# Decayed attention and a small mixture of experts on one core: another split of keys and queries, other constants, another order of the work

## The chip, the cores and the metric

One core of one Trainium2 chip runs the whole program. The time is the device time of one launch in microseconds (us); a kernel's time is the median of its runs. TensorE is called PE here, its weight loads PEld, VectorE DVE, ScalarE ACT, GpSimd POOL, and the queue that issues every transfer of this kernel SP.

## The reference

There are 8 batches, 8 heads, 576 positions and a head size of 64. First comes causal attention with a decay per position, then a mixture of four small attention experts on its result, of which each position uses two:

```
scores = q @ k.T / 8                                    # per batch and head, 576 x 576
cum    = cumsum(log(clip(f, 1e-4, 1)))                  # decay of the head
scores = where(j > i, -1e9, scores + cum[i] - cum[j])
attn   = softmax(scores) @ v                            # x: 8 x 576 x 512, heads side by side

logits = x @ w_gate ; top-2 of 4 experts, softmax over the two -> w
for e in 0..3:
    qe, ke, ve = x @ wq[e], x @ wk[e], x @ wv[e]
    ye = softmax(causal(qe @ ke.T / 8)) @ ve @ wo[e]
    out += w[e] * ye          where e is one of the two
```

## The kernel before, in words

The unit of work is a pair: two heads of a batch (32 pairs, kind "a") or two experts of a batch (16 pairs, kind "m"). Products are made exact enough by splitting each operand into a rounded high part (type fp32r, made by an ACT copy) and a low part (the rest, made by a DVE subtraction); a product is high times high plus the two mixed ones.

A pair goes through these tasks. Each is a Python generator; each `next` on it emits the instructions up to its next `yield`, and that is called a step.

- `prep_attn` (L372): loads keys and queries of both heads from DRAM into `xin` (one transfer of 576 KB into 64 of the 128 partitions; the two halves of `xin` alternate from pair to pair), rounds the keys and the queries with two ACT copies into 64 partitions ("near") of the tile `kq` (L380), reads two or three rows of constants, decay and -1 into the other 64 partitions ("far") of `kq` (`extra_rows`, L358), makes the two low parts with DVE into the tile `ka` (L387), and copies the two high parts into `ka`, to the partitions where its second matmul operand needs them, with two transfers of 288 KB (`copy_bits`, L370). There are four `kq` buffers and three `ka` buffers.
- `max_pass` (L536): an approximate product (high parts and far rows of `kq` alone, contraction over 128 partitions) for the maximum of each row. PE writes blocks of scores to two PSUM buffers (L546), DVE reduces them (L552, L565), PE turns the ten columns of maxima into rows (`mp`, L609), ACT negates them (L612), and two small transfers write them into one far row of `kq` (`ms`, L370). Only then can the scores start.
- `scores` (L639): exact scores by two matmuls a block, `ka` (L643) and `kq` (L644), in two PSUM buffers; ACT takes the exponential (L660 to L698), POOL zeroes what lies above the diagonal (L630, L663, L700) and adds up the rows for the softmax sums (L706 to L712).
- `attend` (L721): 14 matmuls (28 in the trace, since plain fp32 is done in two passes; L731) of values and probabilities.
- per two pairs `row_sums` (L762) and `apply_rows` (L813) divide by the sums. For a batch's experts come besides `moe_front` (values and gate, L422), `prep_moe` (keys and queries of the experts, L518) and `project_out` (L864), whose result SP stores.

At the start there are `decay_rows` (the logarithms and their cumulative sum), `spread_rows` (writes the rows of decay and constants to a DRAM table `ex`, from which `extra_rows` reads all pairs but the first), `load_weights` (nine pieces of the experts' weights, three steps each: load, ACT copy, POOL subtraction, L346) and `constants` (POOL).

What sets the order is a string, `ORDER`. Two of its digits (base 64) name a task in a list of 292; the tasks are advanced by one step each time their number stands in the string, 5285 steps in all. At the end every instruction is bound to follow the one emitted before it on its engine (L925 to L930). So each engine, and SP's queue of transfers, does its work strictly in the string's order, and an instruction that waits holds up everything behind it on its own engine; engines run ahead of each other as far as data and buffers allow.

`warm` (L182) multiplies a tile of zeros, to no effect on the result. 35 such products stand at the very start (L271 to L274). More are bound to steps of the first three pairs (`WARM`, L380 and L387): those are emitted right behind the copy or subtraction of `prep_attn` and wait for it (`together`).

Of the kernel before, what the change touches and what calls it, by code (L numbers as in the profile page):

```python
# [11 lines left out]
F32 = mybir.dt.float32  # L12
F32R = mybir.dt.float32r
# [38 lines left out]
1b1f1f1d1p1p1f1f1f16161b1b1b1b1b1b1b1b1b1b1b161m1m1m1m1k1k1k1k1l1p1w1y1p1p1p0q1p1p1p1p1p1p1m1m1p1m1m1m1p0c1b1c1c
1g1g1g1g1g1g17171m17171g1g1m1k1k171l1c1m1m0i1m1g1g1g1g1g1g1g1p1p1p1k1k1m1m1717171w1g1g1g0Q1g1g1g1g1g1g1m1k1x171m
161m1p1p1m1m1m1p1p1p1p1w1p1p1p1p1p1g1g1g1p1p1g1g1g1g0u1m1m1m1p1m1m1w1p1h1h1q1q1q1q1p0X0X1q1w1q1w1w0X0X1n17171n1n
1n1n1p171h1q1q1q1i1i1q1i1q1B1q1i1i171i1n1n1n1q1n1n1i0b0b1q0X0X1n0X0X1n1q1i1n1n1n1i1q1q0X0W1n1n1n1n1q1q1q1I1q1q1n
1n1n1n1n1n1y1n1n1n1n1n1j1j0X0X1q1q1q1q1q1j1y1B1y1B1x1B1o1B1o1y1n1r1r1r1y1y1y1y1N1B1B1D1r1r1r0X0X1i1y1j1j1y1y1y1y
1r1r1r1r1y1r1r1o1y1y1r0V1y1y1y1r0X0X1y1y1y1j1j1r1r1r1r1r1r1r1r1r1r1r1r1r1D1D1C1y0W1y1r1y1D1I1j1r1r1j1j1j1y1D1D1I
1D1r1j1D1c1D1s1j1D1z1D1D1D1D1z1z1z1z1I1z1D1z1D1D1z1z1z1I1z151K1K1K1z1z1K1t1t1D1D1z1z1z1z1D1D1D1D101s1U1U1U1U1K1t
1t1t1s1K1N1t1t1U1U1z1z1z1z1z1z1t1z1z1z0U1D1D1J1t1U1U1U1U1U1U1U1U1V1D1I1D1D1U1U1U1m1t1U1K1U1U1U1U1U1K1K1U1z1u1u1E
1E1E1E1E1N1z1N1N1u1u1K1K1K1K1K1u1u1u1z1u1E1E1E1A1u1u1u1N1E1E1E1K1K1U1U1E1E1E1u1u1E1q1E1I1I1K1U1U1U1K1K1K1d1K1z1z  # L60
1i1U1V1V1K1K111U1V1V1E1U1U1U1U1U1U1U1U1u1u1u1u1N1V1E1E1V1E1E1E1E1E1K1K1K1E1E1E1E1E1A1A1W1V1V1E1K1E1V1P1P1N1U241V
1V0+1V1V1F1F1P1P1V1V1F1P1V1V1V1V1V1V1K1V1P1P1P1P1V1w1V1V1V1L1L1L1L0X1o1L1P1P1L1P1P1U1G1G1V1L1V1O1P1P1G1G1P1P1P1L
1L1L1L1L1G1L1L1L291G1P1P1P1V1P1V1P1V1L1V1V1V1V1L1L1L0L1P1P1P1Z1P1P1G1G241L1L1L1L1L1L1L0n1Z1Z0A1Z1W1G1V1Z1W1W1U1U
# [64 lines left out]
def tile_decay_attention_moe(ctx: ExitStack, tc, qk, v, f, w_gate, wq, wk, wv, wo, out):  # L128
    nc = tc.nc
# [52 lines left out]
    def warm(at, cols, after=None, n=None):  # L182

        for i, r in enumerate(at):
            k = slice(r, r + (n or 128 // len(at)))
            mm = nc.tensor.matmul(wps[i][:, :cols], wz[k, 0:128], wz[k, :cols], start=True, stop=True)  # L186
            if after is not None:
                together(mm, after)
# [25 lines left out]
    for _ in constant_rows(0, nc.vector):  # L214
        pass
# [756 lines left out]
```

## Time and profile before

| | |
|---|---|
| median of 3 runs | 722.81 us (721.54 to 724.28) |
| the profiled execution | 721.82 us, its span 719.9 us |
| PE busy | 687.3 us, 95% of the span, 5373 instructions |
| DVE busy | 575.9 us, 80% |
| POOL busy | 469.3 us, 65% |
| ACT busy | 445.2 us, 62% |
| transfers | 72.81 MB, mean 101 GB/s |
| mean granted PE clock | 0.981 |

The span runs from the first to the last instruction. Matmuls are pipelined, so a stretch in which PE is busy throughout need not be a stretch at its full rate; the time in which PE stands idle, and what ended the idle time, is read from the stretches and from the timeline. The granted clock of a stretch is given as a share of 2.4 GHz.

### The profile page before, as it was taken

The page shows a single profiled execution, that of the slowest core. Times are in us where ns is not written, and L with a number is a line of the kernel's source. Part 1 is how long each engine was busy: PE and PEld are TensorE (multiplying, and loading weights), DVE is VectorE, ACT ScalarE, POOL GpSimd, SP SyncE. Part 2 cuts the span into 40 slices and gives each one's busy share as a digit, 9 for nine tenths or more (in the row PEclk, how much of TensorE's full clock was granted, in tenths as well). Part 3 has the DMA queues.
Part 4 walks back from the last instruction along what each step waited for, and adds up shares of the span by engine and source line. Part 5 has one row for each costly group of instructions (what it writes and reads, how often), then busy time and mean ns, then how long its engine had stood idle before and what let it go on. Part 6 is the DMA issues. An engine that isn't in the chain of part 4 may idle for free.

```text
span 719.9 us, 15408 instructions
## 1 busy us (share of the span) xinstructions
PE 687.3 (95%) x5373; PEld 559.8 (78%) x5373; DVE 575.9 (80%) x1666; ACT 445.2 (62%) x959; POOL 469.3 (65%) x767
## 2 busy tenths in 40 slices
PE   8788899999999999999999999999999999999997
PEld 4466688768787798788878788877988788979864
DVE  6678976897888888897988888788987987866662
ACT  4465756666576665676576765766666675556443
POOL 8799864687556865766655946667657776465270
PEclk9588999999999999999999999999999999999999
DMA  7756343362254425263262643353444324112103
GB/s 166 204 117 177 78 112 94 73 157 54 57 135 113 122 54 135 55 166 96 56 159 74 155 88 103 69 146 99 106 118 102 101 73 100 39 48 64 34 30 117
DMA packets 29469, 72.81 MB, mean 101 GB/s; under 512 B 4169, under 2 KB 4649, under 8 KB 27345
## 3 DMA queue, kind: packets, MB, share of 16 engines
q1 hardware_dynamic: 29393, 71.84, 40.3%
q8 instruction: 42, 0.69, 0.4%
q14 instruction: 34, 0.28, 0.1%
HBM read 32.91 MB, written 10.35 MB: 60 GB/s over the span
## 4 chain that ended last, share of the span: by engine, by line
PE 68%; POOL 10%; DVE 9%; ACT 5%; DMA 4%; issue 3%; SPq 0%; POOLq 0%; DVEq 0%; ACTq 0%
PE pp_m L518 10%; PE pv L422 7%; PE ob_a L731 6%; PE s_a L643 6%; PE m_a L546 5%; PE po L864 5%; PE s_a L644 5%; PE s_m L643 4%; PE m_m L546 3%; PE s_m L644 3%; PE oa_a L731 3%; POOL R_m L706 3%; PE sm_a L771 2%; PE warm L186 2%; POOL R_m L708 2%
## 5 line engine op out<-in xcount | busy, mean ns | idle before, releaser
L630 POOL TENSOR_SCALAR_AFFINE_SELECT P_a<-P_a 128x128 f32<-128x128 f32 x128 | 45.9, 361 | 107.0 <-ACT P_a L693 59.6
L552 DVE CUSTOM_DVE_ANT_0 junk_a<-m_a,mask 128x320 bf16<-128x320 f32 (+2 forms) x192 | 93.2, 485 | 26.6 <-PE m_a L546 18.2
L643 PE MATMUL s_a<-ka_a 128*128 128x320 f32 (+4 forms) x384 | 111.1, 313 | 1.5 <-ACT P_a L660 0.9
L644 PE MATMUL s_a<-kq 128*128 128x320 f32 (+4 forms) x384 | 104.6, 299 | 0.7 <-DMA kq<-ms_a 0.7
L546 PE MATMUL m_a<-kq 128*128 128x320 f32 (+4 forms) x384 | 93.4, 316 | 7.2 <-DVE mxs_a L552 4.0
L387 DVE TENSOR_TENSOR ka_a<-xin,kq 64x1152 fp32r<-64x1152 f32 x64 | 96.2, 1503 | 2.5 <-ACT kq L380 1.0
L526 ACT ACTIVATE kq<-pp_m 64x288 fp32r<-64x288 f32 x128 | 51.8, 405 | 62.6 <-DVE ka_m L528 43.4
L528 DVE TENSOR_TENSOR ka_m<-pp_m,kq 64x288 fp32r<-64x288 f32 x128 | 58.3, 455 | 34.5 <-ACT kq L526 32.4
L643 PEld LDWEIGHTS s_a<-ka_a 128*128 128x128 f32 (+1 forms) x384 | 70.9, 185 | 14.6 <-ACT P_a L660 4.6
L380 ACT ACTIVATE kq<-xin 64x1152 fp32r<-64x1152 f32 x64 | 73.0, 1157 | 11.1 <-DMA xin<-in_qk_dram 10.4
L706 POOL TENSOR_TENSOR R_a<-P_a 128x448 f32<-128x448 f32 x64 | 78.7, 1230 | 0.0
L546 PEld LDWEIGHTS m_a<-kq 128*128 128x128 f32 (+1 forms) x384 | 63.9, 186 | 18.1 <-DVE mxs_a L552 8.0
L644 PEld LDWEIGHTS s_a<-kq 128*128 128x128 f32 (+1 forms) x384 | 70.5, 185 | 1.8 <-DMA kq<-ms_a 0.9
L731 PE MATMUL ob_a<-P_a,va 128*64 128x320 f32 (+1 forms) x512 | 68.8, 411 | 0.0
L708 POOL TENSOR_TENSOR R_a<-R_a,P_a 128x320 f32<-128x320 f32 x64 | 65.2, 1019 | 4.9
L660 ACT ACTIVATE P_a<-s_a 128x512 f32<-128x512 f32 x64 | 36.6, 597 | 34.7 <-PE s_a L644 33.8
L643 PE MATMUL s_m<-ka_m 128*128 128x192 f32 (+2 forms) x192 | 54.7, 309 | 1.1 <-ACT P_m L660 0.9
L731 PEld LDWEIGHTS ob_a<-P_a,va 128*64 128x64 f32 x512 | 36.4, 140 | 24.9 <-issue 1.4
L552 DVE CUSTOM_DVE_ANT_0 junk_m<-m_m,mask 128x192 bf16<-128x192 f32 (+2 forms) x96 | 46.5, 485 | 9.3 <-PE m_m L546 6.3
L644 PE MATMUL s_m<-kq 128*128 128x192 f32 (+2 forms) x192 | 51.3, 294 | 1.5 <-DMA kq<-ms_m 1.5
L663 POOL TENSOR_SCALAR_AFFINE_SELECT P_a<-P_a 128x256 f32<-128x256 f32 x64 | 32.5, 519 | 30.9 <-ACT P_a L660 30.2
L630 POOL TENSOR_SCALAR_AFFINE_SELECT P_m<-P_m 128x128 f32<-128x128 f32 x64 | 19.7, 310 | 44.4 <-ACT P_m L678 29.8
(189 smaller groups left out, 2069.8 us busy)
## 6 DMA issues: line engine op xcount, KB each, us to landing
xin<-in_qk_dram SPq DMA_DIRECT2D x32, 576.0 KB
ka_a<-kq SPq DMA_DIRECT2D x64, 288.0 KB
va<-in_v_dram SPq DMA_DIRECT2D x32, 320.0 KB
ka_m<-kq SPq DMA_DIRECT2D x32, 288.0 KB
out_dram<-outb SPq DMA_DIRECT2D x32, 256.0 KB
kq<-ex SPq DMA_DIRECT2D x47, 27.0 KB
kq<-ms_a SPq DMA_DIRECT2D x64, 2.5 KB
out_dram<-outb SPq DMA_DIRECT2D x8, 128.0 KB
```

The costliest lines, as they stand in the source:

```text
L380: made = nc.scalar.activation(hi[near], x[:, 2 * c : 2 * c + 2], AF.Copy)
L387: made = nc.vector.tensor_tensor(lo, x[:, 2 * c : 2 * c + 2], hi[near].bitcast(F32), ALU.subtract)
L518: nc.tensor.matmul(pp[:, :HS], w[:, c, es], x[c][:, gs], start=(n == 0), stop=(n == 3 * KC - 1))
L528: nc.vector.tensor_tensor(lo[:, h, gs], src, hv.bitcast(F32), ALU.subtract)
L546: nc.tensor.matmul(dst, qB[0:K, h, i0 : i0 + dst.shape[0]], kB[0:K, h, j0:j1], start=True, stop=True)
L552: nc.vector.tensor_tensor_reduce(jk[:, :n], src, mask[:, MW - n :], 1.0, init, ALU.add, ALU.max, acc)
L630: return nc.gpsimd.affine_select(pv, pv, [[1, 128]], ALU.is_ge, 0.0, base=0, channel_multiplier=-1)
L643: nc.tensor.matmul(dst, kaf[:, c : c + m], qA[:, h, i0:i1], start=True, stop=False)
L644: nc.tensor.matmul(dst, kqf[0:K, c + h * S : c + h * S + m], qB[0:K, h, i0:i1], start=False, stop=True)
L706: g.tensor_tensor(r[:, h, 128:S], q[:, 320:768], q[:, 768:1216], ALU.add)
L708: g.tensor_tensor(r[:, h, 256:S], r[:, h, 256:S], q[:, 1216:1536], ALU.add)
L731: mm = nc.tensor.matmul(dst[64 * h : 64 * h + 64, c0 : c0 + rhs.shape[-1]], vs[h][0:kp, blk], rhs, start=first, stop=last,)
```

## The change

- Layout. The host lays out keys and queries of a pair as 128 rows of two heads: for one pair the keys in rows 0 to 63 and the queries in rows 64 to 127, for the next the other way round, so that keys land in the pair's near rows and queries in its far rows. `xin` becomes a tile of the pool `work` with two buffers.
- High parts. ACT rounds the keys into `kq` (near) as before, and the queries now into `ka` (far). The queries' place in `kq` (near) is filled from `ka` by ACT for the first two pairs (`NACT`), and by a transfer of 288 KB for all others. This transfer stands ahead of `extra_rows`; the second one, keys from `kq` to `ka`, stays at the end.
- Constants. The rows of -1 are set for the first pair's `kq` alone. The selectors `sel` are written directly by memsets; eight `affine_select`s, the buffer they used (shared with `max_pass`) and two DVE copies go.
- Zero products. `warm` and `WARM` go. A task `keep_warm` with 50 products of zeros (bf16, 128 x 128 by 128 x 512) takes their place, one a step, which the order can put anywhere; they wait for nothing but the memset of their operand.
- `junk`, which DVE's reductions write and nobody reads, gets a second buffer.
- `ORDER` is another string: 293 tasks, 5328 steps.

```
-ORDER (5285 steps)   4w4w4w4z004z02054x4w4w4w4y00004x4x0000...
+ORDER (5328 steps)   004x4x4x4x004w4x00004y4y4y4y4y4A4A4y4x...
-WARM = (1, 1, 1)
+NWARM = 50
+NACT = 2
...
-    xin = const.tile([128, 4, S], F32, name="xin")
...
+    wz = const.tile([128, 512], BF16, name="wz")
+    nc.vector.memset(wz, 0.0)
+
+    def keep_warm():
+        wps = ptile(ps_o, "o", "warm")
+        for _ in range(NWARM):
+            nc.tensor.matmul(wps, wz[:, 0:128], wz, start=True, stop=True)
+            yield
...
-        nc.gpsimd.memset(kq[far.start : far.start + 2, :, 1].bitcast(F32), -1.0)
-
+        if i < DIRECT:
+            nc.gpsimd.memset(kq[far.start : far.start + 2, :, 1].bitcast(F32), -1.0)
...
-            sf = work.tile([128, 128], F32, tag="mx0", name=f"self{p}")
-            nc.gpsimd.memset(sf, 0.0)
+            nc.gpsimd.memset(sel[p].bitcast(F32), 0.0)
             for h in range(2):
-                blk = sf[:, 64 * h : 64 * h + 64]
                 base = 32 * (2 * p + h)
-                for r in range(2):
-                    nc.gpsimd.affine_select(
-                        blk, blk, [[0, 64]], ALU.not_equal, 1.0, base=-(base + r), channel_multiplier=1
-                    )
-                    yield
-            yield
-            nc.vector.tensor_copy(sel[p], sf)
-            yield
+                nc.gpsimd.memset(sel[p][base : base + 2, 64 * h : 64 * h + 64].bitcast(F32), 1.0)
+                yield
...
-        x = xin[near]
+        x = work.tile([128, 2, S], F32, tag="xin", name="xin" + nm, bufs=2)
         nc.sync.dma_start(x, qk[b, hp])
         yield
-        for c, hi in ((1, kB), (0, qB)):
-            made = nc.scalar.activation(hi[near], x[:, 2 * c : 2 * c + 2], AF.Copy)
-            if u["first"] is not None:
-                for _ in range(WARM[u["first"]]):
-                    warm((0, 64), 512, made)
+
+        for hi, at in ((kB[near], near), (qA[far], far)):
+            nc.scalar.activation(hi, x[at], AF.Copy)
             yield
+        if u["i"] < NACT:
+            nc.scalar.activation(qB[near], x[far], AF.Copy)
+        else:
+            copy_bits(qB[near], qA[far])
+        yield
         yield from extra_rows(u, b * NPH + hp)
-        for c, hi, lo in ((1, kB, kA[far]), (0, qB, qA[near])):
-            made = nc.vector.tensor_tensor(lo, x[:, 2 * c : 2 * c + 2], hi[near].bitcast(F32), ALU.subtract)
-            if u["first"] is not None:
-                for _ in range(WARM[u["first"]]):
-                    warm((0,), 512, made)
+        for lo, hi, at in ((kA[far], kB[near], near), (qA[near], qA[far], far)):
+            nc.vector.tensor_tensor(lo, x[at], hi.bitcast(F32), ALU.subtract)
             yield
         copy_bits(kA[near], kB[near])
         yield
-        copy_bits(qA[far], qB[near])
-        yield
...
-            jk = work.tile([128, MW], BF16, tag="junk", name="junk" + nm)
+            jk = work.tile([128, MW], BF16, tag="junk", name="junk" + nm, bufs=2)
```

Read by tasks, the two orders begin like this (steps of a task in brackets; "a0_0" is batch 0, pair 0):

- before, on PE: 35 zero products, then `max_pass` a0_0 with the zero products of pairs 0, 1 and 2 in between, the first block of a0_1's `max_pass`, `mp` of a0_0, more of a0_1, `scores` a0_0. On DVE the subtractions of pair 1 stand behind the first of the two 448-column reductions of a0_0, those of pair 2 behind the second one of a0_1. On SP: `f`, a weight, pair 0, pair 1, then the table `ex`, the decay rows of pair 0, and the rest.
- after, on PE: 36 zero products, all blocks of `max_pass` a0_0, 12 zero products, the first block of a0_1, `mp` of a0_0, more of a0_1 with one zero product, `scores` a0_0. On DVE the subtractions of pair 1 stand behind the 320-column reduction of a0_0, those of pair 2 behind the one of a0_1. On SP: `f`, pair 0, two weights, pair 1, two weights, the decay rows of pair 0, then the table `ex`. On POOL the subtractions of all weights and the last constants stand ahead of the third mask of a0_0's `scores`; before, three weight subtractions and the last constants stood behind the scores of a0_0.
- from batch 1 on, the same tasks follow each other in nearly the same sequence; the steps within them are placed differently.

## Rows read from the trace of the kernel before

**Rows 1.** Busy time by stretch: PE, PEld, DVE, ACT, POOL, clock, DMA share, GB/s

```profile
13.90:26.10 12.20, 7.54 (x25) 4.26 (x24) 8.15 (x24) 2.22 (x2) 8.45 (x11) 0.65 0.99 238
...
40.80:88.40 47.60, 42.27 (x297) 29.57 (x296) 41.38 (x107) 30.40 (x62) 42.90 (x67) 0.93 0.56 135
90.00:684.00 594.00, 581.97 (x4750) 488.70 (x4748) 491.00 (x1461) 379.68 (x834) 378.26 (x629) 1.00 0.39 96
```

**Rows 2.** Timeline of PE: start, length, engine, line, tiles, count, idle before

```profile
13.77 0.87 PE L546 MATMUL m_a<-kq 128*128 128x192 f32 x4
...
19.71 0.80 PE L186 MATMUL warm<-wz 128*128 128x512 f32 x1 [2.69 <-DVE ka_a L387]
...
29.77 0.36 PE L643 MATMUL s_a<-ka_a 128*128 128x192 f32 x1
...
40.81 0.87 PE L731 MATMUL oa_a<-P_a,va 128*64 128x256 f32 x8
...
88.40 0.87 PE L731 MATMUL oa_a<-P_a,va 128*64 128x256 f32 x8
```

**Rows 3.** The chain of work in order of time, from its start to 27 us

```profile
1.53 12.45 PE warm L186 x36
...
15.17 7.29 DMA xin<-in_qk_dram
22.49 2.22 ACT kq L380 x2
24.76 0.79 PE warm L186 x2
...
26.33 0.23 PE mp_a L609
```

**Rows 4.** The same chain at its end

```profile
709.37 6.83 PE po L864 x27
```

**Rows 5.** Zero products by their shapes, 1.5 to 13.9 us

```profile
L186 PE MATMUL warm<-wz 128*128 128x512 f32 x8 | 5.2, 731 | 1.5 <-DVE wz L179 1.5
```

**Rows 6.** Timeline of DVE

```profile
14.54 0.36 DVE L552 CUSTOM_DVE_ANT_0 junk_a<-m_a,mask 128x192 bf16<-128x192 f32 x1 [2.23 <-PE m_a L546]
...
17.50 0.63 DVE L552 CUSTOM_DVE_ANT_0 junk_a<-m_a,mask 128x448 bf16<-128x448 f32 x1
...
18.30 2.74 DVE L387 TENSOR_TENSOR ka_a<-xin,kq 64x1152 fp32r<-64x1152 f32 x2
...
23.08 0.49 DVE L552 CUSTOM_DVE_ANT_0 junk_a<-m_a,mask 128x320 bf16<-128x320 f32 x1
```

**Rows 7.** Timeline of SP, which issues the transfers

```profile
9.31 0.66 SPq L295 DMA_DIRECT2D ex<-chl  x1
10.01 1.42 SPq L362 DMA_DIRECT2D kq<-chl  x2
...
26.87 1.66 SPq L370 DMA_DIRECT2D kq<-ms_a  x2
```

**Rows 8.** Busy time in stretches of 2 us, columns as in rows 1

```profile
36.00:38.00 2.00, 1.95 (x8) 1.37 (x7) 0.68 (x4) 1.68 (x5) 2.00 (x5) 0.50 0.58 135
...
52.00:54.00 2.00, 2.00 (x12) 1.27 (x14) 1.97 (x4) 0.36 (x1) 1.92 (x2) 0.50 0.07 19
```

**Rows 9.** POOL's groups from 0 to 45 us: busy, mean ns, idle before

```profile
L238 POOL TENSOR_SCALAR_AFFINE_SELECT self<-self 128x64 f32<-128x64 f32 x8 | 5.5, 705 | 0.4
L212 POOL MEMSET kq<- 2x1152 f32 x4 | 4.2, 1051 | 0.2
```

**Rows 10.** POOL's groups from 40.8 to 88.4 us

```profile
L346 POOL TENSOR_TENSOR ol<-st_o,oh 128x512 fp32r<-128x512 f32 x2 | 2.5, 1272 | 0.0
L346 POOL TENSOR_TENSOR ql<-st_q,qh 128x512 fp32r<-128x512 f32 x1 | 1.3, 1283 | 0.0
```

**Rows 11.** Who waited for whom: us in total, times, longest

```profile
SPq L874 <- ACT outb L871: 51.6, 18, 15.0
...
PE s_m L644 <- DMA kq<-ms_m: 1.5, 1, 1.5
```

More of the change, by code (lines that the diff above doesn't have):

```diff
@@ new lines @@
+080d0e0e0j0e0j0j0808080j0e0e0e0j0j0t0j0e0j090j0e0f0o0o0o0o0o080o0o0f0j0j0j0j0f0f0f0f0f0j0j0f0j0f0f0f0j0j0j0j0f0f
+0j0j0a0a0a4z0j0j0j09090a0a0q0a0a0f0f0f0f0j0j0a0q0F0q0q0f0f0f0f0f0f0f0f0f0f0f0q0a0q0q0k0b0q0t0k0f0t0b0b0b0k0i0k0k
+0q0t0t0g0g0t0t0b0q0q0q0q0k0k0k0k0k0k0k0k0q0u0k0k0g0b0f0b0q0q0q0v0k0k0k0q0q0k0k0k0k0k0k0k0k0k0k0k0k0k0q0q0A0q4y0q
+0t0v0b0v0v0b0b0q0q0q0q0b0A0v0v0A0f0A0A0v0p0v0v0A0l0v0C0v0v0v0v0b0b0r0r0r0r0r0l0l0v0v0A0r0r0r0v0r0v0v0v0v0v0r0r0r
+0F0m0m0m0m0m0m0r4w0r0r0r0r0r0r0r0r0r0r0r0r0r0r0r0p0r0r0v0v0v0v0v0m0v0A0m0m0C0C0F0C0M0M0F0C0C0s0F0F0n0w0n0n0n0w0s
@@ new lines @@
+0n0C0C0C0n0n0w0w0w0w0w0w0n0n0C0C0C0C0w0M0w0w0C0w0w0n0n0n0w0w0w0C0w0w0C0s0C0w0w0N0N0N0n0C0C0w0N0w0w0w0r0C0N0C0F0H
+0w0w0w010N0H0N0N0x0C0w0w0C0w0C0C0C0M0H0H0N0N0N0N110x0M0M0N0N0N0C0C000N0Y0w0F0N0N0N0N0N0N0N0N0N0N0N0N0H0B0D0D0D0H
+0H0H0H0N0N0N0N0N0N0N0N0N0M0x0M0M0M4z0M0H0H0H0D0M0D0H0H0N0y0G0y0y0O0O0y0y0H0H0D0M0M0M0M0O0y0y0y0D0D0D0D0D0H0H0M0H
+0H0y0M0M0M0D0D0R0Z0D0D0H0M0M0M0b0H0D0D0H0M0M0M0M0M0M0M0M0M0M0M0D0D0M0M0M0M0H0H0H0R0R0Z0R0R0D0M0R0M0M040O0R0D0D0D
+0R0D0D0M0D0D0D0D0R0H0R0R0R0D0D0R0R0R0R0R0O0O0O0O0O0+0R0G0I0I0I0I0E0E0O0O0O0O0z0z0z0z0I0I0O0I0Y0O0O0I0z0I0R0R0I0I
@@ L127, in tile_decay_attention_moe @@
+4v4v4v4v4v4v4v3S
+"""
+NWARM = 50
+NACT = 2
 @with_exitstack
@@ L176, in tile_decay_attention_moe @@
     kqs = [const.tile([128, 2, 2, S], F32R, name=f"kq{i}") for i in range(NKQ)]
-    xin = const.tile([128, 4, S], F32, name="xin")
-    wz = const.tile([128, 512], F32R, name="wz")
-    nc.vector.memset(wz.bitcast(F32), 0.0)
-    wps = [ptile(ps_o, "o", f"warm{i}") for i in range(2)]
[L182 to L188, printed above, removed]
+    wz = const.tile([128, 512], BF16, name="wz")
[5 more added lines that the diff above has]
+            yield
     def together(ins, other):
@@ L211, in constant_rows @@
         yield
-        nc.gpsimd.memset(kq[far.start : far.start + 2, :, 1].bitcast(F32), -1.0)
+        if i < DIRECT:
+            nc.gpsimd.memset(kq[far.start : far.start + 2, :, 1].bitcast(F32), -1.0)
+    DIRECT = 1
     for _ in constant_rows(0, nc.vector):
@@ L269, in tile_decay_attention_moe @@
     nc.vector.memset(neg, -1.0)
-    full, halves_, low_half = ((0,), 512), ((0, 64), 512), ((0,), 512, None, 64)
-    thin = ((0, 64), 128)
-    for args in 3 * [full] + 4 * [halves_] + 3 * [low_half] + 6 * [thin] + 3 * [full, halves_]:
-        warm(*args)
     def decay_rows():
@@ L889, in tile_decay_attention_moe @@
     for i, (kind, b, p) in enumerate(seq):
-        u = dict(kind=kind, b=b, p=p, i=i, nm=f"_{kind}{b}_{p}", first=i if i < len(WARM) else None)
+        u = dict(kind=kind, b=b, p=p, i=i, nm=f"_{kind}{b}_{p}")
         if p % 2 == 0:
@@ L909, in tile_decay_attention_moe @@
                 tasks.append(lambda g=grp, b=b: project_out(g, b))
+    tasks.append(keep_warm)
     tasks.append(decay_rows)
@@ L938, in turned @@
     def turned(x):
-        return x.reshape(b, p, 2, s, d).transpose(0, 1, 4, 2, 3)
-    qk = np.concatenate([turned(q), turned(k)], axis=3)
+        return x.reshape(b, p // 2, 2, 2, s, d).transpose(0, 1, 2, 5, 3, 4)
+    q, k = turned(q), turned(k)
+    qk = np.stack([np.concatenate([k, q], axis=3)[:, :, 0], np.concatenate([q, k], axis=3)[:, :, 1]], axis=2)
+    qk = qk.reshape(b, p, 2 * d, 2, s)
     blocks = -(-s // 128)
```

181 lines of the change are left out of this document (85 added, 96 removed).

## The prediction

> **What bounds the kernel now.** I read the stretches first, then PE's timeline, then the chain of waits, then the other engines' timelines. From 90 to 684 us PE is busy for 581.97 of 594 us [rows 1]: it bounds the kernel there, and only 12.0 us of idle time are visible. From the first `attend` (40.81) to the fifth (88.40) [rows 2] PE is busy for 42.27 of 47.60 us, and POOL for 42.90 [rows 1]: two engines share the bound, and 5.3 us of PE are idle. Before that PE mostly waits. From 13.9 to 26.1 us it is busy for 7.54 of 12.2 us, part of it with zero products [rows 1]. So time can come from three places: the start, the 47.6 us behind it, and the 12.0 us spread over the rest.
>
> What holds the start is seen in the chain [rows 3]: 36 zero products end at 13.98; then the load of pair 2 (issued at 15.17, 7.29 us), its two ACT copies (22.49, 2.22 us), two zero products bound to them (24.76), and only then `mp` of pair 0 at 26.33. A product that computes nothing makes the maximum of pair 0 wait for the load of pair 2. PE's timeline shows the same before: 2.69 us idle until 19.71, for a zero product bound to DVE's subtraction of pair 1 [rows 2].
>
> **The change part by part.** Changes against the profiled execution are meant.
>
> *First `max_pass` product (13.77 before [rows 2]).* Two things release it. The decay rows: SP issued the write of the table `ex` at 9.31 and the rows at 10.01 [rows 7]; with the rows first, they are issued at 9.3. From the issue of the `ms` transfers at 26.87 [rows 7] to the scores at 29.77 [rows 2] it took 2.9 us, so the rows can be there at 12.2. The zero products ahead: 36, starting at about 1.4. No row shows one in bf16. Below stands 0.25 us each, from 27 products of 512 columns in 6.83 us at the high clock [rows 4]: 1.4 + 9.1 = 10.5, when the decay rows decide, at 12.2. Above stands 512 columns at 1.2 GHz, 0.43 each: 16.8. I take the nearest row, 36 pieces in 12.45 us [rows 3], 0.35 each: 13.9. Change 0.1, so 0 (from -1.6 to +3.0).
>
> The full-size zero products took 731 ns each from issue to end [rows 5], the pieces 0.35 us from one to the next [rows 3] against 0.25 late in the run [rows 4], and at 36 to 38 us the granted clock is 0.50 [rows 8]: the start runs, at least in part, at 1.2 GHz. The Trainium skill ("TensorE: Matmul & The Clock Gate", "Part 1: The HAM clock gate") says that half rate is the default and that activity releases it. By that rule the back-to-back bf16 products get the high clock before the 36 are done, and the first product comes nearer 12.2 than 13.9: 1.7 us better than what I take.
>
> *From there to `mp` (12.56 us before: 13.77 [rows 2] to 26.33 [rows 3]).* No product waits for pair 1 or 2 any more. What is left is DVE's work, from [rows 6]: 0.77 to the first reduction (14.54), 3.59 to the end of the first of 448 columns (17.50 + 0.63), 0.63 for the second, 0.49 for one of 320, 2.74 for the subtractions of pair 1, and 1.0 for the small ones and the last of 320 (0.49 again). That is 9.2, with 0.8 for the passing between engines 10.0. Change -2.6. What can be late next is the subtraction of pair 1's queries: its ACT copy stands behind a weight copy whose load stands behind three writes of the table. If that takes as long as before, the change is 0; without the 0.8 it is -3.4. `mp` to scores stays at 3.4 (29.77 - 26.33).
>
> Beside this: the 12 zero products between a0_0's last block and a0_1 take 3.0 (0.25 each) to 5.2 us (0.43), beside the 2.74 and the reductions behind them; without that cover they cost up to 2.4. The third ACT copy (1.11, half of 2.22 [rows 3]) of pair 0 lies under the wait for the decay rows, that of pair 1 under ACT's wait; uncovered 1.1. POOL saves eight selections (5.5 us) and three memsets (3 x 1.05) [rows 9]; POOL is ahead of its first mask anyway, so 0. The second `junk` is 0 too: DVE works in order.
>
> *From the scores of a0_0 to the fifth `attend`.* The 11.0 us from 29.77 to 40.81 [rows 2] I leave: half clock (0.50 at 36 to 38 us [rows 8]) and the same tasks. In the next 47.6 us POOL loses three weight subtractions, 3.8 us [rows 10], which now stand before; PE has 5.3 us of idle time, and some stretches are at 0.50 (52 to 54 us [rows 8]), where 2 us of busy PE are worth 1. POOL's floor falls to 39.1. I take -3.0, a little over half the idle time; bounds -5.3 (all of it) and +2.0 (two more such stretches of 2 us).
>
> *The steady part.* Every pair has the same matmuls, reductions and exponentials. Transfers: two of 288 KB a pair as before, one less for the first two pairs. What differs is the spacing. I counted, in both strings, PE's work (columns at 2.4 GHz) between the last use of a score buffer, a maximum buffer or a last reduction and the next product that needs it, from pair 6 on: under 1.0 us at 80 + 60 + 11 = 151 places before, 65 + 52 + 7 = 124 after, 18% fewer. 18% of the 12.0 us are 2.1. I take -2.0; bounds 0, and -6.0 if as much again hides in products that run slower than their columns. The last 12 us of PE's work are the same products, with one moved: 0.
>
> Sum: 0 - 2.6 - 3.0 - 2.0 = -7.6, so 721.82 - 7.6 = 714.2 for an execution like the profiled one. The median of the runs lies 1.0 above that one: 715.2, say 715.
>
> **The rivals.**
>
> *The queries come late (slower).* For 30 of 32 pairs the queries' place in `kq` is now filled by a transfer instead of ACT, and `extra_rows` stands behind it on SP. `max_pass` cannot start before, and all of PE is queued behind its first product. Price: from issue to reader 2.9 us for 2.5 KB (above), 7.29 for 576 KB with others in the queue [rows 3]; for 288 KB I take 5. In the new string the transfer stands 2.0, 2.2, 3.0, 3.8 and 3.8 us of PE's work ahead of its reader in five of the 26 attention pairs from pair 6 on, and 4.3 to 5.9 in six more. Against 5 that lacks 10.2 and 1.4 us: 12, with no gain in the steady part: 715 + 2 + 12 = 729. It decides where the real lead falls under 5 us. For it speaks that SP can be held up by the instruction before (stores waited 51.6 us for ACT, 15.0 at the longest [rows 11]). Against it: SP goes on as soon as that one is released, wherever the step stands, and counted from the ACT copy the five leads are 6.7 to 9.1 us. Before, PE lost 1.5 us to the `ms` transfer of an expert pair, once [rows 11].
>
> *The zero products hold the start.* At 0.43 each the first product comes at 16.8 and the 12 later ones cost their 2.4 uncovered: +3.0, and up to +5.4. 715 + 3 to 5.4: 718 to 720.5. For it: the 731 ns [rows 5]. Against it: 0.35 a piece before [rows 3], most of them 512 columns wide.
>
> *The start is given back.* POOL's 39.1 us and the half clock set the pace to the fifth `attend` whenever it begins, so the first two gains are lost: 721.8 - 2.0 + 1.0 = 721, no change.
>
> *More comes.* The idle time to the fifth `attend` goes wholly and the hidden waits count: -2.6 - 5.3 - 6.0 = -13.9, so 709.
>
> **How the numbers follow.** Forecast 0.46 (own range 711 to 719), more 0.18, zero products 0.14, given back 0.12, late queries 0.10. A measurement of this kernel tells 0.5%, 3.6 us, from no change: under 719.2 is faster, over 726.4 slower. Faster: 0.46 + 0.18 + 0.06 of the zero products' case = 0.70; same: 0.08 + 0.12 = 0.20; slower 0.10. The range 705 to 724 holds the forecast, the cases of given back and of zero products and most of "more", and leaves out the late queries and what goes beyond the bounds.
>
> **What would show it.** First `max_pass` product between 12.2 and 16.8; `mp` of a0_0 about 10 us later; scores of a0_0 at 27 instead of 29.77; no wait of a product of zeros on ACT or DVE. First to fifth `attend` in 44 to 45 us, and no POOL weight subtraction in it. From 90 to 684 us about 10 us of PE idle. Wrong: waits of `m_a` products on a transfer into `kq` of more than 2 us in total; a low granted clock beyond 70 us; the fifth `attend` not before 86.

## The result, and the profile after

The changed kernel takes 711.45 us (median of 4 runs, 710.51 to 712.05) against 722.47 beside it (721.54 to 724.28): a ratio of 0.9843, 95% interval 0.9821 to 0.9866. Its profiled execution took 711.69 us with a span of 709.9, so 10.1 us less than the one before. 715 had been forecast.

Two stretches of the changed kernel, columns as in [rows 1]; the one from 20 to 32 us is used further down:

```profile
20.00:32.00 12.00, 8.46 (x29) 5.58 (x28) 6.94 (x22) 7.75 (x10) 6.92 (x10) 0.63 0.65 177
...
90.00:684.00 594.00, 581.83 (x4774) 490.07 (x4774) 486.11 (x1465) 379.26 (x841) 382.40 (x637) 1.00 0.36 94
```

Read the last line beside its partner in [rows 1]. PE's idle time is the same, 12.2 us against 12.0. But 4774 matmul records stand where 4750 stood, since the changed kernel is further ahead at the end of the stretch than at its start. Over equal work, from the fifth `attend` to the 46th, PE is idle for 12.0 us in both: the same products go by faster, and the idle time that the profile counts is in sum the same.

Timeline of PE, the events of [rows 2] and some new ones:

```profile
1.26 10.33 PE L185 MATMUL warm<-wz 128*128 128x512 bf16 x36 [1.26 <-DVE wz L180]
11.24 0.93 PE L530 MATMUL m_a<-kq 128*128 128x192 f32 x4
...
21.63 0.27 PE L593 MATMUL mp_a<-ident,mxs_a 128*10 128x128 f32 x1
23.62 1.06 PE L530 MATMUL m_a<-kq 128*128 128x192 f32 x3 [1.72 <-ACT ms_a L596]
...
26.58 0.72 PE L627 MATMUL s_a<-ka_a 128*128 128x192 f32 x1
...
38.07 0.87 PE L715 MATMUL oa_a<-P_a,va 128*64 128x256 f32 x8
...
82.67 0.87 PE L715 MATMUL oa_a<-P_a,va 128*64 128x256 f32 x8
```

The first `max_pass` product comes at 11.24 instead of 13.77, `mp` at 21.63 instead of 26.13 (PE's timeline; the chain of [rows 3] enters it at 26.33, where the product before it ends), the scores at 26.58 instead of 29.77, the first `attend` at 38.07 instead of 40.81, the fifth at 82.67 instead of 88.40 [rows 2]. So 5.7 us of the 10.0 are gained by the fifth `attend`; it is shown below that this is not the whole of it.

The chain of waits at the start, beside [rows 3]:

```profile
18.36 7.87 DMA xin_a<-in_qk_dram
26.26 1.16 ACT kq L367
27.44 1.16 ACT ka_a L367
28.63 0.64 ACT oh L330
...
31.86 5.37 DMA ka_a<-kq
...
37.87 0.27 PE mp_a L593
38.14 0.80 PE oa_a L715 x8
```

No zero product stands in it any more, and `mp` of pair 0 doesn't wait for the load of a later pair (what it still waits for is shown in the part on the prediction). That load is still in the chain; it has moved one event on and now ends in front of the second `mp` (37.87) and the first `attend`. The chain of the third pair, and the table of waits, show the transfer that PE still waits for:

```profile
47.19 0.28 ACT ms_a L596
...
48.34 0.37 SPq L363
...
48.81 4.12 DMA kq<-ms_a
```

```profile
PE s_a L628 <- DMA kq<-ms_a: 1.2, 2, 0.8
```

(SP issues a load of 576 KB, L363, between the two small writes of `ms`.) No wait of an `m_a` product on a transfer into `kq` is among the PE rows. The stretch at the low clock and the two stretches of [rows 8], columns as in [rows 1]:

```profile
23.20:36.90 13.70, 11.80 (x40) 8.90 (x40) 7.11 (x19) 8.79 (x16) 8.01 (x11) 0.50 0.65 179
...
36.00:38.00 2.00, 1.28 (x7) 1.01 (x6) 0.77 (x3) 1.75 (x3) 1.29 (x3) 0.79 0.12 33
52.00:54.00 2.00, 1.20 (x10) 1.02 (x8) 1.33 (x5) 0.79 (x2) 1.92 (x2) 1.00 0.96 214
```

The granted clock is 0.50 (1.2 GHz) from 23.2 to 36.9 us and then full (2.4 GHz) for the rest but the last 2.7 us; before, it was still low at 52 to 54 [rows 8].

### The profile page after: what moved, and what is told of

Its sections match the earlier page's. It is cut to its first block, busy times and chain, and to the rows that moved or that the text cites. A ratio compares the mean times of both kernels' runs of the same rounds, so it can differ in the third digit from the quotient of the medians.

```text
span 709.9 us, 15289 instructions
## 1 busy us (share of the span) xinstructions
PE 679.3 (96%) x5369; PEld 554.2 (78%) x5370; DVE 565.0 (80%) x1664; ACT 447.4 (63%) x961; POOL 463.5 (65%) x760
## 4 chain that ended last, share of the span: by engine, by line
PE 71%; POOL 11%; DVE 7%; DMA 4%; ACT 4%; issue 3%; SPq 1%; ACTq 0%; POOLq 0%; DVEq 0%
PE pp_m L502 11%; PE pv L406 8%; PE ob_a L715 6%; PE s_a L627 6%; PE po L848 6%; PE m_a L530 6%; PE s_a L628 5%; PE m_m L530 3%; PE s_m L627 3%; PE ob_m L715 3%; PE s_m L628 3%; PE sm_a L755 3%; PE oa_a L715 2%; POOL R_a L690 2%; DMA xin_a<-in_qk_dram 2%
## 5 line engine op out<-in xcount | busy, mean ns | idle before, releaser
L536 DVE CUSTOM_DVE_ANT_0 junk_a<-m_a,mask 128x192 bf16<-128x192 f32 (+2 forms) x192 | 91.3, 486 | 22.6 <-PE m_a L530 19.7
L530 PE MATMUL m_a<-kq 128*128 128x320 f32 (+4 forms) x384 | 90.5, 314 | 8.4 <-ACT ms_a L596 4.5
L510 ACT ACTIVATE kq<-pp_m 64x288 fp32r<-64x288 f32 x128 | 51.9, 405 | 67.6 <-DVE ka_m L512 39.7
L690 POOL TENSOR_TENSOR R_a<-P_a 128x448 f32<-128x448 f32 x64 | 85.4, 1334 | 0.0
L627 PEld LDWEIGHTS s_a<-ka_a 128*128 128x128 f32 (+1 forms) x384 | 70.7, 184 | 10.2 <-ACT P_a L644 2.8
L692 POOL TENSOR_TENSOR R_a<-R_a,P_a 128x320 f32<-128x320 f32 x64 | 61.7, 964 | 4.6
L376 DVE TENSOR_TENSOR ka_a<-xin_a,kq 64x1152 fp32r<-64x1152 f32 x32 | 48.8, 1524 | 4.6 <-ACT kq L367 3.7
L536 DVE CUSTOM_DVE_ANT_0 junk_m<-m_m,mask 128x192 bf16<-128x192 f32 (+2 forms) x96 | 45.8, 484 | 8.2 <-PE m_m L530 7.1
L694 POOL TENSOR_TENSOR R_a<-R_a,P_a 128x192 f32<-128x192 f32 x64 | 48.5, 758 | 4.5
L376 DVE TENSOR_TENSOR ka_a<-xin_a,ka_a 64x1152 fp32r<-64x1152 f32 x32 | 48.7, 1521 | 2.1 <-ACT ka_a L367 1.2
```

Source lines behind the costliest of these rows:

```text
L376: nc.vector.tensor_tensor(lo, x[at], hi.bitcast(F32), ALU.subtract)
L530: nc.tensor.matmul(dst, qB[0:K, h, i0 : i0 + dst.shape[0]], kB[0:K, h, j0:j1], start=True, stop=True)
L536: nc.vector.tensor_tensor_reduce(jk[:, :n], src, mask[:, MW - n :], 1.0, init, ALU.add, ALU.max, acc)
L627: nc.tensor.matmul(dst, kaf[:, c : c + m], qA[:, h, i0:i1], start=True, stop=False)
L690: g.tensor_tensor(r[:, h, 128:S], q[:, 320:768], q[:, 768:1216], ALU.add)
L692: g.tensor_tensor(r[:, h, 256:S], r[:, h, 256:S], q[:, 1216:1536], ALU.add)
```

## The experiments

To compare the runs in one table, I took the start of the n-th `attend` in PE's timeline (of 48; the last two follow each other closely and count as one, so n ends at 47) and subtracted it from that of the kernel before: the lead in us. "Layout" is the place and width of keys and queries, "order" the string.

| run | layout | order | ratio (95%) | n=1 | n=5 | n=12 | n=32 | end |
|---|---|---|---|---|---|---|---|---|
| changed kernel | new | new | 0.984 (0.982-0.987) | 2.7 | 5.7 | 2.7 | 10.2 | 10.0 |
| e2 | old | old | 0.994 (0.991-0.996) | 3.7 | 5.7 | 2.5 | 2.7 | 2.8 |
| e5 | old | new | 0.996 (0.995-0.997) | 0.1 | 0.6 | -2.5 | 3.1 | 4.0 |
| e6 | old | new to n=5, then old | 1.003 (1.001-1.004) | 0.1 | 1.8 | -0.1 | 0.9 | 0.5 |
| e7 | old | old, zero products unbound | 0.998 (0.996-0.999) | 1.4 | 2.4 | 0.9 | 0.8 | 1.0 |
| e8 | new | new, no zero products | 0.988 (0.986-0.991) | 5.3 | 8.6 | 1.2 | 7.8 | 8.3 |
| e9 | new | old | 1.019 (1.015-1.022) | 2.5 | 0.0 | -7.0 | -13.6 | -13.4 |
| e10 | new | new, loads by pairs | 0.985 (0.982-0.988) | 4.0 | 5.6 | 2.7 | 10.2 | 10.6 |
| e11 | new | new, writes together | 0.984 (0.982-0.987) | 4.6 | 6.4 | 3.1 | 10.6 | 11.2 |
| e12 | new | old, maxima first | 1.022 (1.018-1.025) | -3.7 | -3.3 | -14.7 | -16.6 | -16.3 |

(Before, the 5th is at 88.4 us, the 12th at 187.6, the 32nd at 466.5. The leads are those of one profiled execution each; the ratios are of all runs.)

**The parts alone (e1 to e4).** e1 undoes the layout alone:

```diff
-        x = work.tile([128, 2, S], F32, tag="xin", name="xin" + nm, bufs=2)
+        x = xin[near]
         nc.sync.dma_start(x, qk[b, hp])
...
-        for hi, at in ((kB[near], near), (qA[far], far)):
-            nc.scalar.activation(hi, x[at], AF.Copy)
-            yield
-        if u["i"] < NACT:
-            nc.scalar.activation(qB[near], x[far], AF.Copy)
-        else:
-            copy_bits(qB[near], qA[far])
+        for c, hi in ((1, kB), (0, qB)):
+            nc.scalar.activation(hi[near], x[:, 2 * c : 2 * c + 2], AF.Copy)
+            yield
...
         copy_bits(kA[near], kB[near])
+        copy_bits(qA[far], qB[near])
```

> The new order, constants and zero products, but keys and queries loaded into 64 partitions, rounded by ACT into kq, and the queries copied from kq to ka by the second transfer, as before. Theory A (the order and the zero products make the gain): 711 to 714, the fifth attend at 82 to 84 us. Theory B (the layout makes it: faster loads, fewer stalls on SP): 717 to 722.

736.88 us, ratio 1.0206 (1.0174 to 1.0237): far above all that was expected. The new order loads nine pairs ahead of the one before them (the fourth pair of batch 1 before the third, as the first), and the old `xin` has its two halves bound to even and odd pairs. Such a load can overwrite a half still to be read: by the strings it stands ahead of copies or subtractions of the pair that has the half for six pairs in e1, five in e4 and one in e3, whose scores are then computed from another pair's keys and queries. So e1 says nothing clean of the layout.

e2 has the old layout and the old order too (its digits put into the changed kernel's tasks, 36 zero products in front and 14 behind the first `max_pass`, none bound):

```diff
-004x4x4x4x004w4x00004y4y4y4y4y4A4A4y4x4x4y4y4A4A4A054A4A4A4w4A4A4A004A004z4w4w4w4w4y4w4w4w4w4w4w4w4w4w4w4w4w4w4w
+4w4w4w4w4w4w4w4w4w4w4w4w4w4w4w4w4w4w4w4w4w4w4w4w4w4w4w4w4w4w4w4w4w4w4w4x4x4x4A004A02054y4x4x4x4z0000004y4y0000
...
```

> As the first run, but with the order of before (36 zero products in front, 14 behind the last block of the first max_pass, none bound to a copy). Theory A: most of the gain is gone, but what the bound zero products cost comes back: 718 to 721, the fifth attend at 85 to 88. Theory B: as the first run, 717 to 722. If the zero products alone make the start: the fifth attend at 83.

718.59 us, 0.9937 (0.9914 to 0.9961). The fifth `attend` is at 82.67 here as well, so the unbound zero products and the other constants together bring as much of a start as the whole change does (unbinding alone brings 2.4 us there, e7 below; the rest was not taken apart); but 3.2 of the 5.7 us are gone by the twelfth, and from there the lead doesn't move any more.

e3 joins the new start to the old rest, e4 the old start to the new rest, both with the old layout:

```diff
-0F0m0m0m0m0m0m0r4w0r0r0r0r0r0r0r0r0r0r0r0r0r0r0r0p0r0r0v0v0v0v0v0m0v0A0m0m0C0C0F0C0M0M0F0C0C0s0F0F0n0w0n0n0n0w0s
+0F0m0m0m0m0m0m0r4w0r0r0r0r0r0r0r0r0r0r0r0r0r0r0r0p0r0r0v0v0v0v0v0m0v0A0m0m0C0C0F0C0M0M0F0C0C0s00010j0a4z4z0g0F0F
...
-0v0v0m0m0m0m0l0r0r0r0r0r0v0r0r0r0m0r0r0r0v0v4x0F0F0m0C0C0v0v0v0C0C0m0m0m0F0F0F0F0r0r0s0n0n0n0n0w0w0n0w0m0C0C0w0w
+0v0v0m0m0m0m0l0r0r0r0r0r0v0r0r0r0m0r0r0r0v0v4x0F0F0m0C0C0v0v0v0C0C0m0m0m0F0F0F0F0r0r0s0i0u4y4w0r0r0p0r0r0A0M0M0C
...
```

(The first pair of lines is e3, from e1's string; the second e4, from e2's. The seam lies behind the fifth `attend`; what is left then follows in the other string's order.)

> As the first run, but the new order only up to the fifth attend, the order of before from there. Theory A with the spacing of the steady part worth 4 us: 715 to 718, the fifth attend as in the first run. If the steady part gained from something other than its order: 711 to 714.

> As the second run up to the fifth attend, the new order from there. Theory A: about 4 us below the second run, 714 to 717. If the order of the steady part is worth nothing: equal to the second run.

728.43 (1.0087, 1.0060 to 1.0114) and 729.70 (1.0107, 1.0071 to 1.0143): both inconclusive, for the reason given for e1. e3 has one of the nine early loads, e4 the other eight, and e6 below, which is e3 without it, took 5.3 us less.

**The same with the loads in the order of the pairs (e5, e6).** The nine pairs of loads that had changed places are put in turn; the rest of the edit is that of e1 and e3:

```diff
-0j0j0a0a0a4z0j0j0j09090a0a0q0a0a0f0f0f0f0j0j0a0q0F0q0q0f0f0f0f0f0f0f0f0f0f0f0q0a0q0q0k0b0q0t0k0f0t0b0b0b0k0i0k0k
+0j0j0a0a0a4z0j0j0j09090a0a0q0a0a0f0f0f0f0j0j0a0q0A0q0q0f0f0f0f0f0f0f0f0f0f0f0q0a0q0q0k0b0q0t0k0f0t0b0b0b0k0i0k0k
...
```

> The first run mended: the new order, with the loads of keys and queries put in the sequence of the pairs, so that none overwrites a half of the buffer that is still read; loads into 64 partitions, queries rounded into kq and copied to ka as before. Theory A (the order makes the steady gain): 711 to 714. Theory B (the layout makes it): 716 to 719, the fifth attend still near 83.

> The third run mended in the same way: the kernel of the fifth run up to the fifth attend, the order of before from there. Theory A: 3 to 5 us above the fifth run, 715 to 718. Theory B: equal to the fifth run within 1.5 us.

e5 took 718.19 us, 0.9960 (0.9945 to 0.9974); e6 723.10, 1.0025 (1.0005 to 1.0044). Two things follow. They share the start and the layout and differ in the order behind the fifth `attend`: 4.9 us by the medians, 3.5 by the spans of the profiled executions (719.4 and 715.9), in which e6 was 1.2 us ahead at the seam, so 4.7 behind it. That is what the new order is worth in the steady part. And e5 differs from the changed kernel mainly in the layout: 6.7 us by the medians, 6.0 by the spans, of which 5.1 are there by the fifth `attend` (lead 0.6 against 5.7). (The kernel before took 721.68 us beside e5 and 722.47 beside the changed kernel, so the medians understate the difference a little.) The chain of e5 shows how:

```profile
19.55 6.48 DMA st_o<-in_wo_dram
26.05 0.63 ACT oh L331
26.68 0.17 ACT ms_a L593
26.86 5.00 DMA kq<-ms_a
...
31.91 0.53 PE s_a L625
```

and its stretch from 20 to 32 us, columns as in [rows 1]:

```profile
20.00:32.00 12.00, 6.25 (x19) 3.06 (x17) 5.37 (x16) 5.40 (x8) 6.32 (x9) 0.64 1.03 223
```

The transfers' engines are full (DMA share 1.03, against 0.65 in the changed kernel), a weight lands late, the ACT copy of the maxima stands behind that weight's copy, and the maxima, two transfers of 2.5 KB, take 5.00 us from issue to reader. SP's timeline of e5 has two transfers of 288 KB into `ka` for each of the first two pairs (16.10 and 21.28) besides its load; with the new layout the third ACT copy takes the place of one of them. Over the whole run PE waits more often for those writes as well:

```profile
PE s_a L625 <- DMA kq<-ms_a: 4.9, 5, 2.1
```

against 1.2 us in the changed kernel.

**The zero products (e7, e8).**

```diff
# e7: the kernel before
-WARM = (1, 1, 1)
+WARM = (0, 0, 0)
# e8: the changed kernel
-NWARM = 50
+NWARM = 0
```

> The kernel before with one edit: no zero products bound to the copies and subtractions of the first three pairs; the 35 in front stay. If the bound ones held the start: mp of a0_0 at 22 to 24, the fifth attend at 82 to 85 instead of 88.4, and 717 to 720. If the constants, the decay rows or the order made the start: fifth attend 87 to 89, 721 to 723.

> The changed kernel with none of the 50 zero products. If they only fill idle time and the clock is low in the first scores anyway: 711 to 713, first scores at 26 to 27. If they are what brings the high clock back by 37 us: low clock to 41 us or beyond, fifth attend 2 to 4 us later, 714 to 717.

e7: 719.75 us, 0.9977 (0.9962 to 0.9993). Unbound, `mp` comes at 24.32 and the fifth `attend` at 86.04, 2.4 us earlier; both are a little short of what was expected if the bound products held the start (22 to 24, 82 to 85), the time is within it, and 1.0 us is left at the end. e8: 712.24 us, 0.9883 (0.9855 to 0.9910), not distinguishable from the changed kernel. Its start is even faster:

```profile
11.02 1.44 PE L530 MATMUL m_a<-kq 128*128 128x192 f32 x4 [11.02 <-DMA kq<-chl]
...
26.23 0.36 PE L627 MATMUL s_a<-ka_a 128*128 128x192 f32 x1
...
79.76 0.87 PE L715 MATMUL oa_a<-P_a,va 128*64 128x256 f32 x8
```

The four products of 192 columns take 1.44 us without zero products ahead and 0.93 with them, so PE is at the high clock there with them and not without; but what follows waits for DVE and for transfers, and with them the granted clock is back at 0.50 from 23.2 us. e8 is granted the full clock from 30.8 us, where its first record stands, but loses it from 85.5 to 88.9 and from 136.7 to 140.1; its lead falls from 8.6 at the fifth `attend` to 1.2 at the twelfth. A start that is 2.9 us faster was worth nothing at the end.

**The layout without the order (e9, e12).** The changed kernel with the order of e2; 16 steps of later pairs stand a little later, since the new buffers would not come free in time. e10 is the changed kernel with the edit of e5's diff alone.

```diff
-004x4x4x4x004w4x00004y4y4y4y4y4A4A4y4x4x4y4y4A4A4A054A4A4A4w4A4A4A004A004z4w4w4w4w4y4w4w4w4w4w4w4w4w4w4w4w4w4w4w
+4w4w4w4w4w4w4w4w4w4w4w4w4w4w4w4w4w4w4w4w4w4w4w4w4w4w4w4w4w4w4w4w4w4w4w4x4x4x4A004A02054y4x4x4x4z0000004y4y0000
...
```

> The changed kernel with the order of the kernel before: full-width loads, halves in two buffers, 36 zero products in front and 14 after the first max_pass; 16 steps of later pairs are put a little later, where the new buffers would otherwise come free too late. Theory A (the layout and the order each bring their own part: from the run with the old layout and the old order, 718.6 us, the layout alone takes what it takes from the start, about 2 us): 715.5 to 717.5, fifth attend at 80 to 83, lead smaller at the end than there. Rival B (the layout is worth the whole 6.7 us by which the changed kernel beats the old layout in the new order, whatever the order): 711 to 713. Rival C (the layout is worth something only in the order made for it): 718 to 720.

> The changed kernel with its loads of keys and queries issued in the order of the pairs, all else as it is. This is the one thing besides the layout in which the run with the old layout and the new order differed. If that run's 718.2 us came of the layout: this one takes 710.5 to 712.5, as the changed kernel. If it came of the order of the loads: 715 to 719.

e10: 711.05 us, 0.9847 (0.9816 to 0.9877). The order of the loads is no cause. e10 and e5 have the same string, so the 6.5 us between them (spans 709.4 and 715.9) are the layout's alone, in this order. e9: 734.97 us, 1.0185 (1.0154 to 1.0215). None of the three theories had the layout alone slower than before. Its chain at the third pair:

```profile
49.13 0.29 PE mp_a L593
49.44 0.27 ACT ms_a L596
49.73 1.17 ACT ka_a L367
50.92 0.63 SPq L356
...
51.60 0.46 SPq L352
...
52.16 3.15 DMA kq<-ms_a
55.36 0.36 PE s_a L628
```

The new transfer (L356) waits for its ACT copy, and the second write of the maxima, which are ready at 49.7, stands on SP behind it and the rows of the table (L352) until 52.1. Its waits and its steady stretch:

```profile
PE s_a L628 <- DMA kq<-ms_a: 8.6, 5, 2.9
PE m_a L530 <- DVE mxs_a L536: 7.8, 9, 2.9
```

```profile
90.00:684.00 594.00, 574.84 (x4645) 480.62 (x4641) 482.89 (x1427) 373.60 (x813) 376.50 (x621) 0.99 0.34 95
```

e12 puts the two writes right behind the ACT copy that makes them (against e9):

```diff
-4w4w4w4y4y0c0c0c02024A074A0702024A0707074A4A4A4A4A4A4A4A4A4A4A4A02004y070707070707070e020703030303030c03074A4A03
+4w4w4w4y4y0c0c0c02024A074A07020202024A0707074A4A4A4A4A4A4A4A4A4A4A4A004y070707070707070e0703030303030c03074A4A03
...
```

> The run of the layout alone, with the two writes of each pair's row maxima issued right behind the ACT copy that makes them, before any other issue on SP. Theory (the layout in the old order is slow because the new transfer of the queries' second half stands on SP ahead of the row maxima and holds them back while it waits for ACT's copies; TensorE waited 8.6 us in 5 places and 2.5 us in 2 for these writes): the waits fall below 3 us, fifth attend at 81 to 84 instead of 88.4, the end 6 to 12 us earlier, 723 to 729. Rival (the old order has ACT's and DVE's new steps in the wrong places; the writes of the maxima are only where it shows): the waits fall, the end 0 to 4 us earlier, 731 to 735.

737.95 us, 1.0217 (1.0183 to 1.0252). The theory falls: the wait of `s_a` for the maxima is not among PE's rows any more, and others have come. The time is above the rival's 731 to 735 as well.

```profile
PE m_a L530 <- DVE mxs_a L536: 9.4, 11, 2.6
PE s_a L627 <- ACT P_a L644: 7.1, 2, 6.9
PE cp_a L805 <- ACT rt_a L789: 6.8, 3, 3.9
```

```profile
90.00:684.00 594.00, 574.93 (x4646) 480.44 (x4644) 484.92 (x1427) 375.40 (x816) 379.92 (x624) 0.99 0.35 96
```

PE's idle time in the steady stretch is 19.1 us in both. Which of the old order's steps stand wrongly for the new layout stays open; that it is not the writes of the maxima alone is shown.

**The writes together (e11).** In the changed kernel, at 19 places, the second write of `ms` is put behind the first, and ACT's copy of an output weight behind the maxima of pair 0:

```diff
-4y4y4A4A4A4A4A4A0502024w4w4w4w4w4w024w4w4w0c4w4A4A4w4w02050707070202020207010707070707070707074w0307070c0c4w4A03
+4y4y4A4A4A4A4A0502024w4w4w4w4w4w024w4w4w0c4w4w4w020507070702024A4A4A020207010707070707070707074w0307070c0c4w4A03
...
```

> The changed kernel with the second write of the row maxima put right behind the first on SP's queue in all 19 places where other issues stood between them, and ACT's copy of an output weight put behind the row maxima of pair 0. Theory (what still lies on the chain of the start is the way from mp to the scores, 4.95 us in the changed kernel and 3.6 before, and the wait of 1.2 us at the scores of the third pair): scores of pair 0 at 25.3 to 25.8 instead of 26.58, the wait gone, fifth attend at 80.5 to 82, the end at 709.5 to 711. Rival (POOL's sums of rows set the stretch to the fifth attend, as the chain shows between 57 and 79 us): scores earlier, but fifth attend at 82 to 83 and the end at 711 to 712. Rival on the other side (loads that are now issued later come too late in the steady part): 712 to 715.

710.49 us, 0.9844 (0.9815 to 0.9874).

```profile
25.70 0.44 PE L627 MATMUL s_a<-ka_a 128*128 128x192 f32 x1
...
81.97 0.87 PE L715 MATMUL oa_a<-P_a,va 128*64 128x256 f32 x8
```

The scores come 0.9 us earlier, the fifth `attend` 0.7, the end 1.1 in the span; the ratio tells it from the changed kernel as little as e10's does. All three lie in the theory's ranges, the fifth `attend` by 0.03 us, and PE's waits have none for the maxima at the third pair any more. But `mp` itself came 1.2 us later (22.82), and of 1.9 us at the first `attend` 0.7 are left at the fifth and 0.4 at the twelfth. So the rival, that the stretch behind takes back most of a better start, is not refuted; theory and rival lie too close for this run to decide.

## Why the prediction was right, and where its steps were not

**First product: forecast no change (-1.6 at best), measured -2.5.** The step had two errors. A zero product took neither 0.35 us nor the 0.25 of the lower bound throughout. Their stretches (L185 alone: PE, PEld, clock, DMA share, GB/s):

```profile
1.30:6.10 4.80, 4.80 (x12) 1.76 (x13) 1.00 0.78 251
6.20:11.20 5.00, 5.00 (x24) 2.25 (x23) 1.00 0.49 178
```

They come 0.43 us apart to 6.1 us and 0.22 apart from there, 1.2 and then 2.4 GHz for 512 columns; the granted clock's first record, 1.00, stands at 6.14. On average that is 0.29 us (10.33 for 36). And the bound by the decay rows, 12.2, was too late, since without zero products the product starts at 11.02, released by those rows (e8). So 11.24 is outside the 12.2 to 16.8 I had given. The rule of the Trainium skill ("TensorE: Matmul & The Clock Gate", "Part 1: The HAM clock gate"), that activity releases the high clock, had the product nearer 12.2 than 13.9; the rows agree with it, by the step from 0.43 to 0.22 us between zero products and by 0.93 us for the first four `max_pass` products, against 1.44 us where nothing stood ahead of them (e8).

**To `mp`: forecast 10.0 us, measured 10.4.** Two errors offset each other. The sum of DVE's pieces, 9.2, held, and the 0.8 for the passing between engines was not needed on top of it. But what could be late was late: DVE stood idle for 1.18 us before the subtraction of pair 1's queries, whose ACT copy stood behind a weight copy, and that one waited for its load.

```profile
17.52 0.63 ACT L330 ACTIVATE kh<-st_k 128x512 fp32r<-128x512 f32 x1 [3.92 <-DMA st_k<-in_wk_dram]
...
19.23 1.53 DVE L376 TENSOR_TENSOR ka_a<-xin_a,ka_a 64x1152 fp32r<-64x1152 f32 x1 [1.18 <-ACT ka_a L367]
```

9.2 and 1.2 are the 10.4. By PE's timeline `mp` stood at 26.13 before, so the change is -2.0.

**`mp` to scores: forecast unchanged at 3.4 (3.6 by PE's timeline), measured 4.95.** This was not examined. ACT's copy of the maxima now stands behind the copy of an output weight, which waits for its load, and PE is idle for 1.72 us behind it. e11 takes this out of the way: 25.70 - 22.82 = 2.9 us. From the scores to the first `attend` it took 11.5 us instead of the 11.0 that I had left as they were. So the start's sum, -2.7 at the first `attend` against the -2.6 forecast, is luck: -2.5, -2.0, +1.3 and +0.5 stand where 0, -2.6, 0 and 0 were forecast.

**First to fifth `attend`: forecast -3.0, measured 47.6 to 44.6, so -3.0.** The size is right, and the POOL floor behind it nearly so; the idle time of which it was taken as a share is not. The same stretch of work in the changed kernel, columns as in [rows 1]:

```profile
38.07:82.67 44.60, 39.75 (x304) 28.71 (x303) 38.76 (x105) 30.57 (x60) 39.59 (x61) 1.00 0.50 133
```

POOL's busy time is 39.6 us instead of 42.9 (forecast 39.1), without any of the three weight subtractions. PE's idle time only falls from 5.3 to 4.9; its busy time falls from 42.3 to 39.8, with the granted clock at 1.00 instead of 0.93. e10 and e11, with the same POOL work (39.7 and 40.2), are at the low clock once more, from 78 to 81 us, and take 45.9 and 45.8 us. So 1.2 to 1.3 of the 3.0 go with the clock of the one profiled execution, and that part is luck; how the rest divides between POOL and the clock was not separated.

**The steady part: forecast -2.0, measured -4.3 (631.5 to 627.2 from the fifth `attend` to the end).** This is the term that was mis-sized. I took it as a share of the 12.0 us of visible idle time, and that hasn't changed. The gain is, for the most part, in products that run slower than their columns. Summed from the `pv` of batch 1 to that of batch 7, what the time from one product's issue to the next's exceeds the columns at 2.4 GHz is 65.0 us instead of 69.5; 3.5 less at the scores of the attention pairs, and small amounts of both signs elsewhere. Visible idle time is in these sums, 7.5 us instead of 8.5, so 57.5 instead of 61.0 lie in slow products. The counting of tight places (18% fewer) pointed the right way, and the pool of time to which it applies was these 61 us besides the 12. But 18% of 61 would be 11 us, so the count gives the direction and not the size. I had put the hidden waits into the lower bound alone. The order is its cause: from the twelfth to the 32nd `attend` the changed kernel and every run with its order and no overwritten keys gain 5.6 to 7.5 us, with either layout (e5, e8, e10, e11), and those with the old one change by -0.1 to 1.0 with the old layout (e2, e6, e7) and lose 6.6 and 1.9 with the new (e9, e12).

**The rivals.** *The queries come late* is refuted for this order: no `m_a` product waits for a transfer. As a mechanism it has a near relation in e9: what the new transfer delays in the wrong order is the write of the maxima behind it on SP; but e12, without that delay, is no faster. *The zero products hold the start* is refuted by 0.29 us a piece and by e8, where the first product comes only 0.2 us earlier without them. *The start is given back* is half true, and I had it at 0.12: of 5.7 us at the fifth `attend`, 2.7 are left at the twelfth, and the e8 row shows 8.6 becoming 1.2. That this is a lead given back is not shown: e5, which leads by 0.6 at the fifth `attend`, loses 3.1 up to the twelfth as well, so the new order may simply be slower there. The total came out well because the steady order's gain, read from the fifth `attend` on, hides it: +7.5 from the twelfth to the 32nd, -3.0 before. *More comes* (709): 711.45 lies between it and the forecast. Its hidden waits are what happened in the steady part; the idle time did not go.

So the forecast was 3.6 us high, in a sum whose start came out by offsetting errors (-2.6 forecast, -2.7 measured at the first `attend`), whose middle held in size, and whose steady term was half of what came.

## What to carry to other kernels

Where a bound engine shows little idle time, also sum what its instructions take beyond their own size: the new order, which gives buffers more distance at 27 places, gained 3.5 us there, where no wait is counted (that the distance is the cause was not tested by itself). A layout and an order made for one another are not two gains to be added (0.994 with the rest of the change alone, 0.996 and 1.019 with one of them, 0.984 with both): price a new layout in the order in which it will run. What stands behind the new transfer on its queue is one thing to look at, but putting that right alone (e12) did not help. And take a gain at the start for its worth some way down the run, not at the end of the start.

## What had not been expected of the hardware

In e8's records the granted clock begins at 30.8 us, and every stretch before reads 1.00; yet its first `max_pass` products, four of 192 columns, took 1.44 us against 0.93 in the changed kernel. In the changed kernel the first record stands at 6.14, the stretch before it reads 1.00 too, and its zero products are 0.43 us apart there against 0.22 behind it. Where no clock record has come yet, the figure says nothing, and spacing has to be read instead.

The first two loads of keys and queries, 64 partitions wide in e5 and 128 in the changed kernel, stand in these stretches, columns as in [rows 1], first of e5, then of the changed kernel:

```profile
3.00:10.00 7.00, 7.00 (x28) 2.91 (x27) 4.54 (x7) 3.77 (x6) 6.63 (x14) 1.00 1.02 239
```

```profile
3.00:10.00 7.00, 7.00 (x27) 2.90 (x26) 5.15 (x7) 4.34 (x6) 6.63 (x14) 1.00 0.76 274
```

Full engines moved 239 GB/s in the narrow form, and engines busy for 0.76 of the time moved 274 in the wide one. The transfers issued are otherwise the same in that stretch, and two more runs with the same issues agree: 239 GB/s at 1.00 in the narrow form (e6), 273 at 0.79 in the wide one (e10). So the wide load costs less engine time for its bytes; no run measured the load by itself.
